# Two query groups per key chunk, and background matmuls in the column tiling of the values

## The chip, the cores and the metric

The kernel runs on one core of one Trainium2 chip. The metric is device time in microseconds (us). Five engines work side by side, each with its own instruction queue in program order: TensorE (PE, its weight loads shown apart as PEld), VectorE (DVE), ScalarE (ACT), GpSimd (POOL) and SyncE (SP), which here issues nearly all DMA transfers.

## The reference, cut to what matters

One transformer layer on x of 1 x 2048 x 640 in bf16: 32 heads of 20, then a gated bilinear feed-forward of width 1728.

```python
h  = x + softmax(q k^T * 20**-0.5) v @ wo      # q, k, v from layernorm(x) @ wqkv
n  = layernorm(h)
h2 = h + ((n @ w_gate) * (n @ w_up)) @ w_down
```

## The kernel before

**Names.** A head's 20 columns are padded to 32, so a group g of four heads fills 128 partitions; there are eight groups (G). A query chunk ci has 512, 512, 512, 256 and 256 queries (`CHUNKS`). A step is one group, one query chunk and 512 columns of scores per head: one key tile of 128 at 512 queries, two at 256. A bank is one head of a step, 128 x 512 scores in PSUM.

**A slot.** The main loop (from L802) runs slot by slot. `emit_exp` puts one ScalarE exponential on three banks, or on two, in turn; `emit_S` puts the score matmuls of a later unit on TensorE, four row tiles of 32; `values` and `emit_PV` multiply finished steps by V, four column tiles of 32 (out partitions 32 j to 32 j + 32, the extra column of ones in Vx giving the softmax sums). Some banks go another way: `start_D` and `pass_D` take the exponential on VectorE and GpSimd (fx, uc, v, ed). When a group's last key tile is through, `normalise` copies the sums (accS), sends them through DRAM to be inverted and spread (rs, rd, rb), and its `third` part writes `on`.

**The background.** Everything else is a generator in the deque `bg`, one matmul at a time, written into what the planner thinks is free TensorE time in a slot. `first_stage` normalizes the input chunk by chunk, transposes it (lnT), and makes K, Q and V: groups 0 and 1 padded (`proj_pad`), groups 2 to 7 densely (`proj_dense`), whose rows go from tmp to kT and qT by DMA on SP; `proj_v` makes V. `second_stage(ci)` is Wo, the second norm, gate and up (14 steps f), and down for a query chunk. Its matmuls are 128 x 128 wide. Generators run strictly one after the other.

**What sets the order.** The instruction order is fixed when the program is built, by running clocks (`pe_t`, `dve_t`, `act_t`), a credit for background work (`rate`) and `m_wait` for two PSUM banks (tag m). `need` breaks out of it: if a tag (a K, Q, V, or ("Wo", ci)) isn't done, it writes background work until it is, whatever the clocks say. A score needs K and Q, `third` of chunk ci needs ("Wo", ci - 1). `debt` writes matmuls of zeros that hold the clock up (L845). After chunk 0, `open_p2` opens the second stage's memory, clears wo on GpSimd and loads wo and Wd.

In chunk 0, group 0 goes through all 16 key tiles, then group 1, and so on:

```python
for g in range(G):
    for k0 in range(0, NT, nk):
        steps.append((ci, q0, qw, g, list(range(k0, k0 + nk))))
```

## Time and profile before

| | |
|---|---|
| median of 2 runs | 1076.33 us (1073.89 to 1078.76) |
| the profiled execution | 1075.21 us, of which the span is 1073.4 |
| mean granted TensorE clock | 0.938 |
| busy: PE, DVE, ACT, POOL | 906.2, 782.1, 865.6, 249.3 us |
| exponentials on ScalarE (L629) | 739, from 19.4 to 1016 us |
| instructions on TensorE in the order | 14,695 rows |

Rows of groups give line, engine, operation, tiles written and read, count, then busy us, mean ns of one, idle time before and what ended it. In a timeline row stand start, length, engine, line and count; in the chain of waits, start, length and what was waited for. A matmul's shape is followed by its tile in the array (rows*columns). Matmuls overlap, so a mean length is not a pace; the distance between starts is.

### The profile page before, as it was taken

What the parts mean: (1) busy time and instruction counts of PE and PEld (TensorE: products, weight loads), DVE (VectorE), ACT (ScalarE), POOL (GpSimd) and SP (SyncE); (2) the same over time, 40 slices, a digit from 0 to 9 for tenths busy, and PEclk for the clock granted to TensorE, in tenths of its full rate; (3) what the DMA queues carried; (4) which work ended last, traced back from release to release, by engine and by line L of the source; (5) the groups of instructions that cost most, each with busy time, mean ns of one, the idle gap of its engine ahead of it and who ended that gap; (6) DMA issues with size and microseconds to landing.
All of it is one profiled execution on the core that took longest, in us unless ns stands there. A gap on an engine that the chain in (4) does not pass through costs nothing.

```text
span 1073.4 us, 19367 instructions
## 1 busy us (share of the span) xinstructions
PE 906.2 (84%) x7249; PEld 349.3 (33%) x7348; DVE 782.1 (73%) x1327; ACT 865.6 (81%) x792; POOL 249.3 (23%) x273
## 2 busy tenths in 40 slices
PE   6778888888875888889888898898888889888968
PEld 2323233222221322233323222233333334434445
DVE  5426685778774899895888899966987886388532
ACT  4568795789884999999998999999968994289801
POOL 3002121222241322222322322222322230122100
PEclk8889799889986999999999999999988999989989
DMA  6200110110142222200012222000202222224145
GB/s 225 57 1 14 28 34 14 32 27 25 35 77 91 49 54 55 51 14 24 24 36 49 48 54 55 17 24 24 65 8 49 48 49 43 56 60 86 30 99 109
DMA packets 126860, 52.05 MB, mean 48 GB/s; under 512 B 108494, under 2 KB 121038, under 8 KB 126766
## 3 DMA queue, kind: packets, MB, share of 16 engines
q1 hardware_dynamic: 126078, 49.73, 19.8%
q8 instruction: 57, 0.93, 0.4%
q10 hardware_dynamic: 432, 0.98, 0.2%
q14 instruction: 37, 0.30, 0.1%
q0 software_dynamic: 256, 0.10, 0.0%
HBM read 43.60 MB, written 2.98 MB: 43 GB/s over the span
## 4 chain that ended last, share of the span: by engine, by line
ACT 39%; PE 24%; issue 18%; DVE 10%; DMA 4%; SPq 3%; POOL 1%; POOLq 0%; DVEq 0%; ACTq 0%
ACT E L629 38%; PE sp L609 6%; PE acc L706 3%; PE mt L547 3%; PE mt L301 2%; PE mt L520 2%; PE mt L360 2%; PE mt L529 2%; PE acc L845 2%; DVE v L662 2%; PE mt L488 2%; DVE ed L667 1%; DVE v L664 1%; SPq L350 1%; DVE st L222 1%
## 5 line engine op out<-in xcount | busy, mean ns | idle before, releaser
L629 ACT ACTIVATE E<-sp 128x1536 bf16<-128x1536 f32 x739 | 844.0, 1377 | 123.0 <-PE sp L609 103.3
L659 POOL TENSOR_SCALAR uc<-fx 128x512 f32<-128x512 uint16 x202 | 179.2, 887 | 584.9 <-DVE fx L656 576.1
L706 PE MATMUL acc<-E,Vx 128*32 128x512 bf16 (+1 forms) x2305 | 207.4, 357 | 5.6 <-DVE accS L720 3.6
L656 DVE TENSOR_SCALAR fx<-mt 128x512 int32<-128x512 f32 x202 | 137.6, 682 | 50.7 <-PE mt L609 49.5
L662 DVE SCALAR_TENSOR_TENSOR v<-fx 128x512 f32<-128x512 uint16 x202 | 168.7, 838 | 2.0
L664 DVE SCALAR_TENSOR_TENSOR v<-v,uc 128x512 f32<-128x512 f32 x202 | 142.9, 709 | 33.4 <-POOL uc L659 28.7
L667 DVE SCALAR_TENSOR_TENSOR ed<-fx,v 128x512 uint16<-128x512 int32 x202 | 143.4, 710 | 2.2
L706 PEld LDWEIGHTS <-Vx 128*32 128x32 bf16 x2560 | 57.3, 95 | 126.6 <-issue 122.2
L520 PE MATMUL mt<-ln2T,wg 128*128 128x512 bf16 (+3 forms) x328 | 83.7, 349 | 4.3 <-DVE ln2T L277 1.9
L529 PE MATMUL mt<-ln2T,wu 128*128 128x512 bf16 (+3 forms) x334 | 83.6, 345 | 2.8 <-issue 1.6
L706 PE MATMUL acc<-ed,Vx 128*32 128x512 bf16 (+1 forms) x255 | 78.9, 354 | 7.0 <-DVE ed L667 6.0
L547 PE MATMUL mt<-Wd,hh 128*128 128x320 bf16 x448 | 81.0, 302 | 1.7 <-DVE ot L552 1.7
L845 PE MATMUL acc<-zeros 128*128 128x512 bf16 x205 | 72.9, 425 | 2.4 <-issue 2.2
L741 POOL TENSOR_TENSOR on<-accS,rb 128x512 bf16<-128x512 f32 (+1 forms) x40 | 48.3, 1207 | 98.2 <-DMA rb<-rd 91.6
L488 PE MATMUL mt<-wo,on 128*128 128x320 bf16 x256 | 50.6, 328 | 19.8 <-POOL on L741 12.8
L535 DVE TENSOR_TENSOR hh<-gs,mt 128x512 bf16<-128x512 f32 (+1 forms) x70 | 40.4, 577 | 25.7 <-PE mt L529 24.6
L547 PEld LDWEIGHTS <-hh 128*128 128x128 bf16 x448 | 39.0, 97 | 40.6 <-issue 27.8
L520 PEld LDWEIGHTS <-wg 128*128 128x128 bf16 (+1 forms) x350 | 29.4, 101 | 40.6 <-issue 30.4
L277 DVE COPY gs<-mt 128x512 f32<-128x512 f32 (+3 forms) x56 | 34.7, 619 | 9.5 <-PE mt L520 8.6
L529 PEld LDWEIGHTS <-wu 128*128 128x128 bf16 (+1 forms) x350 | 29.0, 100 | 38.1 <-issue 27.1
L720 DVE COPY accS<-acc 128x512 f32<-128x512 f32 (+1 forms) x40 | 23.3, 583 | 24.2 <-PE acc L706 24.1
L552 DVE TENSOR_TENSOR ot<-mt,h 128x320 bf16<-128x320 f32 x32 | 15.6, 489 | 34.3 <-PE mt L547 34.2
(135 smaller groups left out, 934.8 us busy)
## 6 DMA issues: line engine op xcount, KB each, us to landing
wg<-in_B_w_gate_dram SPq DMA_DIRECT2D x65, 160.0 KB
wu<-in_B_w_up_dram SPq DMA_DIRECT2D x65, 160.0 KB
rb<-rd SPq DMA_DIRECT2D x24, 256.0 KB
out_dram<-ot SPq DMA_DIRECT2D x16, 160.0 KB
Wd<-in_B_w_down_dram SPq DMA_DIRECT2D x1, 2080.0 KB
rb<-rd SPq DMA_DIRECT2D x16, 128.0 KB
xr<-in_A_x_dram SPq DMA_DIRECT2D x3, 640.0 KB
rs<-accS SPq DMA_DIRECT2D x96, 2.0 KB
```

The source lines that it names most:

```text
L488: nc.tensor.matmul(ps[:, 0:HD], lhsT=On[ci, g][0][:, tt * P:(tt + 1) * P], rhs=wo[:, g, hsl], start=(g == 0), stop=(g == G - 1))
L520: nc.tensor.matmul(pg[0:M, 0:qw], lhsT=wg[:, c, 0:M], rhs=ln2T[:, c, 0:qw], start=(c == 0), stop=(c == KC - 1))
L529: nc.tensor.matmul(pu[0:M, 0:qw], lhsT=wu[:, c, 0:M], rhs=ln2T[:, c, 0:qw], start=(c == 0), stop=(c == KC - 1))
L547: nc.tensor.matmul(ps[:, 0:HD], lhsT=hh[f][0:K, tt * P:(tt + 1) * P], rhs=Wd[0:K, f, hsl], start=(f == 0), stop=(f == NF - 1))
L629: nc.scalar.activation(E[:, 0:len(u), :], sp[:, 0:len(u), :], ACT.Exp, scale=LN2_ / UNIT, bias=-BIAS * LN2_ / UNIT)
L656: nc.vector.tensor_scalar_mul(fx[:], d["sp"][:], 512.0)
L659: nc.gpsimd.tensor_scalar(d["uc"][:], u, EXP_C, 0.0, ALU.mult, ALU.add)
L662: nc.vector.scalar_tensor_tensor(d["v"][:], d["u"], EXP_A, d["u"], ALU.add, ALU.mult)
L664: nc.vector.scalar_tensor_tensor(d["v"][:], d["v"][:], EXP_B, d["uc"][:], ALU.add, ALU.mult)
L667: nc.vector.scalar_tensor_tensor(e[:], d["fx"][:], 1.0 / 512.0, d["v"][:], ALU.mult, ALU.add)
L706: nc.tensor.matmul(acc_t[32 * j:32 * j + 32, 0:qw], lhsT=Vx[:, kt, h * VS:h * VS + 32], rhs=E_of[s, j][0][:, i * qw:(i + 1) * qw], start=( ...
L845: nc.tensor.matmul(acc_t[:], lhsT=zeros[:, 0:P], rhs=zeros[:], start=False, stop=False, skip_group_check=True)
```

## The change

It has these parts.

- `cmm` writes a 128-wide matmul as four matmuls of 32 columns of weights, each into its own 32 partitions. All of the background but the transposes goes through it, the zeros of `debt` too.
- `steps`: in chunk 0, groups 0 and 1 take turns at each 512-key chunk, and accS collects their four partial sums (`ends`, `sums`). `first_stage` makes K of both groups and V of a chunk before the next chunk. While `ingest` holds, no exponential goes to VectorE; `on_act` sends no copy to ScalarE as long as exponentials are left.
- `values` writes two steps at a time (PVS); it also waits for V's copy.
- `third` doesn't call `need` early: it stays in `later` until its tags are done. The two chunks of 256 use two halves of `on` (`O0`, `free_of`), so that chunk 4 needs ("Wo", 0) to ("Wo", 2).
- The rate is RUSH0 = 10 in chunk 0 and while Wo runs (`hurry`); in the last two chunks it counts `more`, the work still to come. `bg` is written to pay `debt`, too, ahead of zeros.
- wo is loaded in `first_stage` over the first input tiles (tag xw), with its zeros by DMA; Wd is loaded in 14 pieces with the weights of chunk 0's second stage; xr and the output share two kept buffers.
- `more_banks` adds the five score banks to the ring of two before the first slot and after the last; 28 warm-up matmuls for 14.

```diff
+    def cmm(out, lhsT, rhs, start, stop, **kw):
+        m = lhsT.shape[-1]
+        for j in range(0, m, 32):
+            nc.tensor.matmul(out[j:j + 32], lhsT=lhsT[:, j:j + 32], rhs=rhs, start=start, stop=stop, **kw)
...
     def on_act(us):
-        return (n_slot < 40 or not left) and act_t + 0.4 < max(dve_t, pe_t)
+        return (not attn or not left or ingest and INGEST_ACT) and act_t + 0.4 < max(dve_t, pe_t)
...
         for ch in range(1, NCH):
-            for t in range(t0, t0 + TPC):
-                yield from proj_v(t, 0)
-                if lns is None:
-                    lns = finish(L, ch)
...
+            lns = finish(L, ch)
+            nxt = stats(ch + 1) if ch + 1 < NCH else None
             for i in range(TPC):
                 yield from transposed(lns[i], lnT_dst(ch * TPC + i))
+            for g in range(NG0):
+                yield from proj_pad(g, ch, 1)
                 if nxt is not None:
                     L = next(nxt)
+            for t in range(ch * TPC, (ch + 1) * TPC):
+                yield from proj_v(t, 0)
...
+        ingest = False
         fill_kq()
+        load_wo()
...
                 for f in range(NF):
-                    K = min(P, FF - f * P)
-                    nc.tensor.matmul(ps[:, 0:HD], lhsT=hh[f][0:K, tt * P:(tt + 1) * P],
-                                     rhs=Wd[0:K, f, hsl], start=(f == 0), stop=(f == NF - 1))
-                    pe(0.135)
+                    cmm(ps[:, 0:HD], hh[f][:, tt * P:(tt + 1) * P], Wd[:, f, hsl], f == 0, f == NF - 1)
+                    pe(0.135, "C")
...
-        for g in range(G):
-            for k0 in range(0, NT, nk):
-                steps.append((ci, q0, qw, g, list(range(k0, k0 + nk))))
+        order = [(g, k0) for k0 in range(0, NT, TPC) for g in range(NG0)] if ci == 0 else []
+        order += [(g, 0) for g in range(len(order) and NG0, G)]
+        for g, k0 in order:
+            k1 = k0 + TPC if ci == 0 and g < NG0 else NT
...
         def third():
-            if ci:
-                need(("Wo", ci - 1))
-            on = onp.tile([P, BK], BF16, name="on", tag=f"on{g}")
+            need(*[("Wo", c) for c in free_of[ci]])
+            on = ons[g]
...
+            if force is None and run == 0 and not ends[s][1]:
+                nxt = range(s, min(s + PVS, len(steps)))
...
-        while later and later[0][0] <= max(dve_t, act_t):
-            later.pop(0)[1]()
+        for z in list(later):
+            if z[0] <= max(dve_t, act_t) and all(t in done for t in z[2]):
+                later.remove(z)
+                z[1]()
...
+            more = sum(W1 * w / BK for w in CHUNKS[ci:-1]) if CHUNKS[ci] < BK else 0.0
             rest = sum(1 for b in left if steps[b[0]][0] == ci or CHUNKS[ci] < BK)
-            rate = RUSH * max(bgw, 5.0) / max(rest / 2.8, 4)
+            rate = RUSH0 if hurry or ci == 0 else RUSH * max(bgw + more, 5.0) / max(rest / 2.8, 4)
...
     values(len(steps))
+    more_banks()
```

Three places show how instructions move. On TensorE, in the down-projection of a chunk (Wd, hh), from the last score (sp) over the value group (acc) to the background (mt), before:

```order
L609 MATMUL sp<-qT_155,kT_151 128x512
L609 LDWEIGHTS kT_152
L609 MATMUL mt<-qT_155,kT_152 128x512
L706 LDWEIGHTS Vx
L706 MATMUL acc<-E,Vx 32x512
...
L547 LDWEIGHTS hh
L547 MATMUL mt<-Wd,hh 128x320
L609 LDWEIGHTS kT_151
L609 MATMUL sp<-qT_155,kT_151 128x512
```

and in the changed program:

```order
L684 LDWEIGHTS kT_150
L684 MATMUL sp<-qT_154,kT_150 128x512
L781 LDWEIGHTS Vx
L781 MATMUL acc<-E,Vx 32x512
...
L146 LDWEIGHTS hh_4780
L146 MATMUL mt<-Wd,hh_4780 32x320
```

Values and background now have one tiling; two value steps stand together, and a background matmul is four, with four loads. TensorE has 26,255 rows for 14,695.

On VectorE, while the last input chunk is normalized (x_101 before, x_100 after): lnT is its transposed copy; kT_146 before and kT_145 after are the keys of group 0, and kT_146 after those of group 1. Before:

```order
L241 RECIPROCAL rstd<-den 128x4
L246 TENSOR_SCALAR x_101<-x_101,mv,rstd 128x640 x4
L277 COPY lnT<-mt 128x5x128 x2
L315 TENSOR_SCALAR kT_146<-mt,kb 128x512
L656 TENSOR_SCALAR fx<-mt 128x512
L662 SCALAR_TENSOR_TENSOR v<-fx 128x512
```

and in the changed program:

```order
L261 RECIPROCAL rstd<-den 128x4
L266 TENSOR_SCALAR x_100<-x_100,mv,rstd 128x640 x4
L796 TENSOR_TENSOR accS<-accS,acc 128x512
L317 COPY lnT<-mt 128x5x128 x4
L354 TENSOR_SCALAR kT_145<-mt,kb 128x512
L796 TENSOR_TENSOR accS<-accS,acc 128x512
L354 TENSOR_SCALAR kT_146<-mt,kb 128x512
L317 CAST Vx<-mt 128x16x20 x4
```

All four transposed copies and the V casts of a chunk are VectorE's, the partial sums of both groups come in between, and the exponentials (fx, v) come later.

On VectorE at the end, from the last copy of sums (accS). Before:

```order
L720 COPY accS<-acc 128x256
L729 RECIPROCAL rr<-rs 128x8
L552 TENSOR_TENSOR ot<-mt,h 128x320 x3
L493 TENSOR_TENSOR h<-mt,xr 128x320 x4
L222 BN_STATS st<-h 128x6 x2
```

and in the changed program:

```order
L794 COPY accS<-acc 128x256
L813 RECIPROCAL rr<-rs 128x8
L317 COPY ln2T<-sp 128x5x128
L607 TENSOR_TENSOR hh_4771<-gs,sp 128x256
...
L607 TENSOR_TENSOR hh_4784<-gs,sp 64x256
L621 TENSOR_TENSOR xr<-sp,h 128x320 x3
L621 TENSOR_TENSOR xr<-mt,h 128x320
L566 TENSOR_TENSOR h<-mt,xr 128x320
```

Before, the end of chunk 3's down-projection (ot) stands behind the last sums, then Wo of chunk 4 (h). Now all 14 steps of chunk 3's gate and up (hh) and its down-projection (xr) stand there ahead of Wo. Behind the last value group TensorE has 1,676 matmuls for 273.

More of the change, by code (lines that the diff above doesn't have):

```diff
@@ L104 @@
     attn = False
+    hurry = False
+    ingest = True
     n_slot = 0
@@ L699, in emit_PV @@
         need(*[("V", kt, g // (G // 2)) for kt in kts])
-        first, last = kts[0] == 0, kts[-1] == NT - 1
+        first, last = ends[s]
         if first:
```

270 lines of the change are left out of this document (170 added, 100 removed).

## The prediction

> **What bounds the kernel now.** I read the page first, for the busy shares.
>
> ```profile
> span 1073.4 us, 19367 instructions
> PE 906.2 (84%) x7249; PEld 349.3 (33%) x7348; DVE 782.1 (73%) x1327; ACT 865.6 (81%) x792; POOL 249.3 (23%) x273
> L629 ACT ACTIVATE E<-sp 128x1536 bf16<-128x1536 f32 x739 | 844.0, 1377 | 123.0 <-PE sp L609 103.3
> ```
>
> TensorE and ScalarE are both near 80 to 85%, so an average names no bound. The third row says what can be lost: 739 exponentials, a slot each, and the idle time before them ends mostly with a score matmul (L609). Next I cut the span at the ends of stages and asked for the busy time and count of those exponentials in each (columns: length, ScalarE busy on that line and count, granted clock, DMA share, GB/s).
>
> ```profile
> 19.40:120.00 100.60, 59.40 (x51) 0.91 0.10 28
> 120.00:319.00 199.00, 168.29 (x147) 0.90 0.15 33
> 319.00:350.00 31.00, 14.76 (x14) 0.67 0.36 97
> 350.00:752.00 402.00, 392.82 (x348) 1.00 0.17 38
> 600.00:750.00 150.00, 150.00 (x134) 1.00 0.16 39
> 752.00:788.00 36.00, 28.76 (x26) 0.95 0.20 50
> 788.00:886.00 98.00, 89.03 (x79) 0.91 0.19 42
> 886.00:934.00 48.00, 14.11 (x14) 0.96 0.24 55
> 934.00:1016.00 82.00, 76.77 (x68) 0.94 0.28 58
> ```
>
> The stretch from 600 to 750 us is the yardstick: ScalarE never stops, 150.00/134 = 1.119 us a slot. Against it each stage loses its length minus 1.119 us times its count: 43.5 us while the input is read and normalized (19.4 to 120), 34.5 in the rest of chunk 0, 15.3 at the handover to chunk 1, 12.6 through chunks 1 and 2, 6.9 and 9.6 around chunk 3, 32.3 between 886 and 934, 5.9 to the end. That is 160.6; slots that cross a border are counted twice (747 for 739), which hides 9 more. So the span is 19.4 (start) + 739 x 1.119 = 827 + 169.6 lost + 57.4 of tail after the last exponential at 1016. ScalarE's pace bounds the middle; the rest is waiting.
>
> The largest wait, from the waits view, ScalarE's timeline and the chain:
>
> ```profile
> ACT E L629 <- PE sp L609: 103.3, 46, 33.9
> 932.45 4.62 ACT L629 ACTIVATE E<-sp 128x1536 bf16<-128x1536 f32 x4 [33.89 <-PE sp L609]
> 904.52 16.90 PE mt L547 x112
> 922.35 4.37 DMA xr<-in_A_x_dram
> 927.35 3.57 PE mt L488 x16
> 933.88 0.33 DVE accS L720
> ```
>
> In chunk 4, `third` needs the whole second stage of chunk 3 up to its Wo; that stands behind chunk 2's down-projection (112 matmuls at 16.90/112 = 0.151 us), so TensorE does it all at once while ScalarE idles 33.89 us.
>
> **The tiling change itself.** TensorE's timeline in a busy stretch (start, length, group):
>
> ```profile
> 501.30 0.39 PE L609 MATMUL sp<-qT_155,kT_152 32*128 32x512 bf16 x2
> 501.62 0.40 PE L706 MATMUL acc<-E,Vx 128*32 128x512 bf16 x4
> 501.95 0.55 PE L547 MATMUL mt<-Wd,hh 128*128 128x320 bf16 x2
> 502.64 0.39 PE L609 MATMUL sp<-qT_155,kT_152 32*128 32x512 bf16 x3
> ...
> 816.60 0.29 PE L706 MATMUL acc<-E,Vx 128*32 128x256 bf16 x2
> 816.60 0.28 PE L706 MATMUL acc<-ed,Vx 128*32 128x256 bf16 x1
> 816.61 0.39 PE L706 MATMUL acc<-E,Vx 128*32 128x256 bf16 x3
> 816.72 0.27 PE L706 MATMUL acc<-ed,Vx 128*32 128x256 bf16 x1
> 816.73 0.71 PE L706 MATMUL acc<-E,Vx 128*32 128x256 bf16 x17
> 817.37 0.39 PE L609 MATMUL sp<-qT_155,kT_149 32*128 32x256 bf16 x4
> ```
>
> Value groups are already four column tiles. Of the 24 from 816.60, the six groups take 0.77 us up to the next score. Four tiles start at one time, since six groups of 256 columns at the full pace of 0.109 us (which I estimate from 256 columns here: 0.77 less one changeover of 0.115, over 6) fit and 24 one behind another would not. A 512-column group is then about 0.216, and from a value group to the next background matmul it is 0.33 (501.62 to 501.95), so a changeover costs 0.33 - 0.216 = 0.115 us. The order has 1,856 changeovers before and 1,434 after: 422 x 0.115 = 48 us less of TensorE. A four-tile background group I price like the 128-wide matmul it replaces, because the value group has the same shape of load and output. But in chunks 1 and 2 ScalarE is busy 392.82 of 402 us, so there the 48 us only become slack. Slack of TensorE is not time.
>
> The Trainium skill speaks against the tiles: TensorEngine Tiling (Array Packing), section Tile-to-Partition Mapping, has column tiling switch off the fast weight load. The value rows carry such loads inside their 0.109 us, so here they stay hidden; if they did not, the result would be the slow rival below.
>
> **What moves, and its price.** The rest of the diff decides.
>
> Start and slots: 19.4 us as now; 740 exponentials for 739: 828.1.
>
> *Input stage (lost 43.5).* Now V casts and transposed copies also run on ScalarE between exponentials, and one group's 16 key tiles use up the chunks as fast as they come. After, VectorE takes all copies, and each 512-key chunk feeds two groups, 12.8 slots, 14.3 us. What stays is a forced lump at each new chunk.
>
> ```profile
> L720 DVE COPY accS<-acc 128x512 f32<-128x512 f32 x24 | 16.6, 690 | 17.3 <-PE acc L706 17.2
> L315 DVE TENSOR_SCALAR kT_147<-mt,kb 128x512 bf16<-128x512 f32 x4 | 3.0, 750 | 0.4 <-PE mt L301 0.3
> L277 DVE COPY lnT<-mt 128x640 bf16<-128x640 bf16 x6 | 3.0, 492 | 26.5 <-PE mt L292 26.5
> ```
>
> In VectorE's order (shown above) that is 0.69 + 4 x 0.492 + 0.75, with five K matmuls of 0.216 and about 0.8 of hops: 5.3 us. ScalarE has two units in hand (2.2), so 3.1 is lost three times, plus 3 to 4 for the clock, 0.91 in this stage: 13.
>
> *Rest of chunk 0 (34.5).* Groups 2 and 4 are scored as soon as their K and Q have passed through SP's queue:
>
> ```profile
> 298.89 4.48 SPq L350 DMA_DIRECT2D qT_155<-tmp  x6
> 1018.84 1.76 DMA rs<-accS
> ```
>
> That is 0.75 each to issue and 1.8 to land. Both early groups now end with the last key chunk, so group 2 waits for nine such issues: 0.9 + 9 x 0.75 + 1.8 = 9.5, less some 4.5 of matmuls planned in between and 2.2 in hand, about 3 to 4. Group 4 waits for 24 forced matmul groups (3.7) and eight issues: 3.7 + 0.9 + 6.0 + 1.8 - 2.2 = 10. The other four starts I take at 1.5 each. Sum 20.
>
> *Handovers.* `third` no longer forces Wo; it waits in `later` until Wo is done, and Wo runs with `hurry`. wo is loaded early and Wd in pieces. 15.3 becomes 5; 12.6, 6.9, 9.6 and 5.9, which hold smaller cases of it, become 9, 5, 8 and 6. Between 886 and 934 chunk 4's outputs lie in the other half of `on`, which only Wo of chunks 0 to 2 frees: 32.3 becomes 0. Lost after: 13 + 20 + 5 + 9 + 5 + 8 + 6 = 66.
>
> *The tail.* It grows. In the order all of chunk 3's feed-forward now stands behind the last value group, ahead of Wo of chunk 4.
>
> ```profile
> 1027.17 5.24 PE L488 MATMUL mt<-wo,on 128*128 128x320 bf16 x25 [2.51 <-POOL on L741]
> 1038.98 1.22 PE L520 MATMUL mt<-ln2T,wg 128*128 128x256 bf16 x5 [0.68 <-DVE ln2T L277]
> 1044.93 0.71 PE L520 MATMUL mt<-ln2T,wg 128*128 128x256 bf16 x5
> 1061.58 8.51 PE L547 MATMUL mt<-Wd,hh 128*128 128x320 bf16 x56
> ...
> 1052.59 4.78 DMA wg<-in_B_w_gate_dram
> ```
>
> Now: 11.2 until Wo, 11.8 to the first gate, 22.6 of gate and up, 8.5 of down, 3.3 to the end: 57.4. Eleven of the 14 steps run from 1044.93 to 1061.58, 1.5 us each. TensorE needs 10 x 0.109 = 1.09 for one, so weights (4.78 us for one transfer) set that pace, and seven PSUM banks instead of two do not mend it. After: 3 (transposes) + 21 + 8.5 for chunk 3, which covers the wait for `on`; then 10.9 (Wo at the full clock) + 21 + 8.5 + 3.3: 76. At TensorE's pace it is 64; with two weight loads in flight at 4.78 us, 2.4 a step, 101.
>
> Sum: 19.4 + 828.1 + 66 + 76 = 989.5, and 1.8 around the span (the profiled run took 1075.21 in all, 0.1% under the median of 1076.33): **992 us**, 8% faster.
>
> **Rivals.**
> (a) The first stages keep their losses: the lumps are serial through VectorE and SP's queue, and one late chunk delays both groups. For it: K and Q of each later group still pass SP one by one. Against: V casts leave ScalarE, and the lumps are short by their rows. Price 43.5 + 34.5 - 33 = 45: 1037.
> (b) The background tiles, with weights that change at every matmul, do not overlap. A group then costs four loads in turn:
>
> ```profile
> L706 PEld LDWEIGHTS <-Vx 128*32 128x32 bf16 x2560 | 57.3, 95 | 126.6 <-issue 122.2
> ```
>
> 4 x 0.095 = 0.38 in place of 0.109 to 0.216. By the order a 512-query stage holds 23 score groups (0.33 with their changeover), 16 value groups (0.216), 23 more changeovers and about 50 background groups (10 us): 23.7 us for ScalarE's 25.7. With 0.38 it is 32.7, +7 in 24 stages, 168. In chunks 3 and 4, 379 groups at +0.25 less their slack, about 62; 419 groups in the tail, 105: 1327, slower. TensorE passes ScalarE from about 0.25 a group on. Against it stands the row of 24 value matmuls.
> (c) TensorE's instruction supply. The program has 13,127 matmuls for 7,347. The densest 4 us stretch I found:
>
> ```profile
> 816.20:820.20 4.00, 3.76 (x64) 1.00 0.00 0
> ```
>
> That is 62.5 ns a matmul; bursts (24 in 0.77) may come out of a filled queue. If 62.5 ns were a limit, chunks 0 to 2 (7,901, 494 us of 621) would not feel it; chunks 3 and 4 (3,550) would need 222 us for 207, +15, and the tail (1,676) 105 for 63, +42: 1049. The Trainium skill, TensorE: Matmul & The Clock Gate, section "Wait — 56ns, not 53.3ns?", gives about 62 ns per matmul for one way of decoding and 25 ns otherwise; no run here shows which holds.
> (d) Losses fall to 40 (the handovers cost almost nothing) and the tail to 64: 954.
>
> **How the numbers follow.** Forecast 0.58, (a) 0.20, (b) 0.07, (c) 0.07, (d) 0.08. The forecast's own spread, 960 to 1025, comes from the tail's bounds and half the losses. The range 950 to 1050 takes in (a), (c) and (d) and leaves out (b) and edges of the others, under 2 in 10. About 2% is what a measurement of this kernel can tell: 1054.8 and 1097.9. Faster: the forecast, (d), nearly all of (a) and half of (c), 0.88. Slower: (b), 0.07. The same: 0.05.
>
> **What would show it.** Slots of 1.12 us in the middle with no wait over 6 us between 400 and 900; ScalarE lost about 13 us before the first dense projection and 10 at group 4; column-tiled groups of 512 starting 0.22 apart; the last exponential near 914; 76 us behind it, with weights as the releaser. I am wrong if background groups start over 0.25 apart, if the input stage still loses 40, or if the tail is far from 76.

## The result, and the profile after

The changed kernel takes 1041.54 us (1041.39 to 1041.69, two runs) for 1076.33: 0.9677 of the time before, 95% interval 0.9582 to 0.9771. Measured again beside other kernels it took 1044.9 us for 1077.62, 0.9687 (0.9657 to 0.9718). It is 3.2% faster where 8% was forecast; the time lies inside the range, 50 us above the forecast.

From the page of the changed kernel, span, busy times and the exponentials, now L704:

```profile
span 1039.9 us, 31066 instructions
PE 868.5 (84%) x13128; PEld 360.1 (35%) x13128; DVE 780.9 (75%) x1328; ACT 861.1 (83%) x784; POOL 234.1 (23%) x268
L704 ACT ACTIVATE E<-sp 128x1536 bf16<-128x1536 f32 x740 | 843.9, 1351 | 81.5 <-PE sp L684 47.7
```

TensorE's busy time fell by 37.7 us, the span by 33.5; both kernels keep TensorE busy 84% of the span. The idle time in front of the exponentials fell by 41.5. The same windows as before, cut at the new ends of stages (length, ScalarE busy on that line and count, granted clock, DMA share, GB/s):

```profile
21.90:109.00 87.10, 61.45 (x53) 0.89 0.18 43
109.00:293.00 184.00, 157.86 (x139) 0.93 0.13 32
293.00:321.00 28.00, 26.28 (x24) 0.94 0.11 35
321.00:726.00 405.00, 390.94 (x345) 0.98 0.19 44
726.00:766.00 40.00, 38.08 (x34) 0.96 0.21 49
766.00:878.00 112.00, 105.26 (x94) 0.92 0.21 46
878.00:942.00 64.00, 64.00 (x57) 1.00 0.15 39
```

The first stretch holds the start of group 2, which ScalarE's timeline shows beside the two waits of group 4:

```profile
106.14 1.02 ACT L704 ACTIVATE E<-sp 128x1024 bf16<-128x1024 f32 x1 [5.92 <-PE sp L684]
166.16 1.02 ACT L704 ACTIVATE E<-sp 128x1024 bf16<-128x1024 f32 x1 [4.96 <-PE sp L684]
172.08 1.45 ACT L704 ACTIVATE E<-sp 128x1536 bf16<-128x1536 f32 x1 [4.89 <-PE sp L684]
```

With 1.119 us a slot, as in the prediction, the sum compares so (lost = length less 1.119 us times count; the 5.9 us of group 2, which end inside the first window, are booked with the rest of chunk 0):

| term, us | forecast | measured | difference |
|---|---|---|---|
| start | 19.4 | 21.9 | +2.5 |
| 740 slots | 828.1 | 828.1 | 0 |
| input stage | 13 | 27.8 - 5.9 = 21.9 | +8.9 |
| rest of chunk 0 | 20 | 28.5 + 5.9 = 34.4 | +14.4 |
| handover 0 to 1 | 5 | 1.1 | -3.9 |
| chunks 1 and 2 | 9 | 18.9 | +9.9 |
| up to 766, up to 878 | 5 + 8 | 2.0 + 6.8 | -4.2 |
| up to the last exponential | 0 + 6 | 0.2 | -5.8 |
| six slots counted twice at borders | 0 | 6.7 | +6.7 |
| tail | 76 | 97.9 | +21.9 |
| span | 989.5 | 1039.9 | +50.4 |

The waits view of ScalarE (total, times, longest):

```profile
ACT E L704 <- PE sp L684: 47.7, 27, 5.9
ACT E L704 <- PE acc L781: 28.1, 20, 3.3
```

The wait of 33.9 us is gone; the longest is 5.9. The second row, exponentials that wait for value matmuls to free their buffers, was 10.3 before.

The tail by its parts: transposes, gate and up of chunk 3, down, Wo and layer norm of chunk 4, its gate and up, its down and the end (busy time of PE, PEld, DVE, ACT, POOL with counts, granted clock, DMA share, GB/s):

```profile
942.00:948.60 6.60, 1.29 (x16) 0.84 (x16) 2.42 (x6) 0.70 (x2) 1.03 (x2) 0.88 0.01 1
948.60:975.10 26.50, 20.07 (x540) 15.84 (x540) 5.52 (x14) 5.20 (x14) 0.73 (x1) 0.90 0.76 151
975.10:984.20 9.10, 8.09 (x236) 6.97 (x239) 1.91 (x5) 0.00 (x0) 0.00 (x0) 1.00 0.06 22
984.20:1001.50 17.30, 7.06 (x137) 4.85 (x127) 6.39 (x17) 0.69 (x1) 0.69 (x1) 0.71 0.41 86
1001.50:1028.00 26.50, 19.23 (x546) 15.99 (x547) 5.47 (x14) 5.20 (x14) 0.00 (x0) 0.93 0.63 133
1028.00:1039.90 11.90, 7.97 (x228) 6.38 (x219) 2.38 (x5) 0.00 (x0) 0.00 (x0) 0.97 0.08 29
```

And its timeline, at the first gate and in the middle of gate and up:

```profile
947.99 0.20 DVE L813 RECIPROCAL rr<-rs 128x8 f32<-128x8 f32 x1 [3.75 <-DMA rs<-accS]
948.11 0.47 DVE L317 COPY ln2T<-sp 128x640 bf16<-128x640 bf16 x1
948.63 1.26 PE L146 MATMUL sp<-ln2T,wg 128*32 128x256 bf16 x20 [3.47 <-DVE ln2T L317]
956.29 0.73 PE L146 MATMUL sp<-ln2T,wg 128*32 128x256 bf16 x20 [0.59 <-DVE hh_4773 L607]
957.49 0.73 PE L146 MATMUL sp<-ln2T,wu 128*32 128x256 bf16 x20 [0.47 <-ACT gs L313]
```

A reciprocal that waits 3.75 us for a transfer stands on VectorE ahead of the copy that the first gate needs. Further on, gate and up matmuls wait for the readers of other matmuls' results.

### The profile page after: what moved, and what is told of

The parts are those of the page before. It is cut to its first block, busy times and chain, and to the rows that moved or that the text cites. A ratio compares the mean times of both kernels' runs of the same rounds, so it can differ in the third digit from the quotient of the medians.

```text
span 1039.9 us, 31066 instructions
## 1 busy us (share of the span) xinstructions
PE 868.5 (84%) x13128; PEld 360.1 (35%) x13128; DVE 780.9 (75%) x1328; ACT 861.1 (83%) x784; POOL 234.1 (23%) x268
## 4 chain that ended last, share of the span: by engine, by line
ACT 37%; issue 25%; PE 18%; DVE 9%; DMA 5%; SPq 3%; POOL 2%; POOLq 0%; DVEq 0%; ACTq 0%
ACT E L704 37%; PE mt L146 7%; PE sp L684 5%; PE acc L781 3%; DMA rb<-rd 2%; SPq L389 2%; PE sp L146 2%; DVE v L737 2%; DVE v L739 1%; DVE fx L731 1%; DVE ed L742 1%; SPq L808 1%; DMA rs<-accS 1%; POOL uc L734 1%; PE acc L146 1%
## 5 line engine op out<-in xcount | busy, mean ns | idle before, releaser
L704 ACT ACTIVATE E<-sp 128x1536 bf16<-128x1536 f32 x740 | 843.9, 1351 | 81.5 <-PE sp L684 47.7
L734 POOL TENSOR_SCALAR uc<-fx 128x512 f32<-128x512 uint16 x198 | 170.2, 860 | 561.9 <-DVE fx L731 555.9
L781 PE MATMUL acc<-E,Vx 128*32 128x512 bf16 (+1 forms) x2312 | 166.5, 352 | 1.9 <-DVE accS L794 1.6
L739 DVE SCALAR_TENSOR_TENSOR v<-v,uc 128x512 f32<-128x512 f32 x198 | 141.7, 717 | 18.8 <-POOL uc L734 14.4
L146 PE MATMUL mt<-ln2T,wg 128*32 128x512 bf16 (+1 forms) x970 | 72.2, 376 | 2.8 <-DVE ln2T L317 1.0
L146 PE MATMUL mt<-ln2T,wu 128*32 128x512 bf16 (+1 forms) x970 | 70.8, 372 | 0.3 <-DVE gs L317 0.3
L146 PE MATMUL acc<-zeros 128*32 128x512 bf16 x696 | 63.1, 420 | 0.0
L146 PEld LDWEIGHTS <-wg 128*32 128x32 bf16 x1350 | 34.5, 99 | 42.7 <-issue 32.7
L146 PEld LDWEIGHTS <-wu 128*32 128x32 bf16 x1350 | 33.6, 98 | 33.3 <-issue 23.6
L684 PE MATMUL sp<-qT_154,kT_146 32*128 32x512 bf16 (+1 forms) x236 | 29.9, 335 | 13.9 <-ACT E L704 13.4
L684 PE MATMUL sp<-qT_154,kT_145 32*128 32x512 bf16 (+1 forms) x223 | 29.0, 343 | 11.4 <-ACT E L704 11.3
L684 PE MATMUL sp<-qT_154,kT_148 32*128 32x512 bf16 (+1 forms) x232 | 29.4, 341 | 10.7 <-ACT E L704 10.5
L794 DVE COPY accS<-acc 128x512 f32<-128x512 f32 (+1 forms) x40 | 23.2, 581 | 19.4 <-PE acc L781 16.9
L684 PE MATMUL sp<-qT_154,kT_152 32*128 32x256 bf16 (+1 forms) x232 | 27.8, 323 | 11.0 <-ACT E L704 10.6
L317 DVE COPY gs<-mt 128x512 f32<-128x512 f32 (+1 forms) x42 | 28.6, 682 | 8.2 <-PE mt L146 8.0
```

Of the source, the lines that this page charges most:

```text
L146: nc.tensor.matmul(out[j:j + 32], lhsT=lhsT[:, j:j + 32], rhs=rhs, start=start, stop=stop, **kw)
L317: nc.vector.tensor_copy(dst, src)
L684: nc.tensor.matmul(out[:, i * qw:(i + 1) * qw], lhsT=kT[g][32 * j:32 * j + 32, kts[i] * P:(kts[i] + 1) * P], rhs=q_of(g, q0, qw)[32 * j:32 ...
L704: nc.scalar.activation(E[:, 0:len(u), :], sp[:, 0:len(u), :], ACT.Exp, scale=LN2_ / UNIT, bias=-BIAS * LN2_ / UNIT)
L734: nc.gpsimd.tensor_scalar(d["uc"][:], u, EXP_C, 0.0, ALU.mult, ALU.add)
L739: nc.vector.scalar_tensor_tensor(d["v"][:], d["v"][:], EXP_B, d["uc"][:], ALU.add, ALU.mult)
```

## The experiments

One table for all runs; the edits follow. The ratio is to the kernel before, measured on the same chip. "Lost" is worked out from each trace: the time between the starts of the exponentials with the numbers given, less 1.119 us for each slot. Slot 60 lies a little behind the start of group 2, slot 195 at the end of chunk 0, slot 560 at the end of chunk 2. The tail runs from the end of the last exponential.

| kernel | median us | ratio (95%) | lost 0-60 | 60-195 | 195-560 | 560-end | tail |
|---|---|---|---|---|---|---|---|
| before | 1076.33 | 1 | 47.8 | 31.5 | 33.1 | 57.5 | 57.6 |
| after | 1041.54 | 0.9677 (0.9582-0.9771) | 28.9 | 30.1 | 20.7 | 12.1 | 97.9 |
| after_again | 1044.90 | 0.9687 (0.9657-0.9718) | 26.2 | 31.3 | 27.6 | 12.1 | 99.9 |
| wide_groups | 1051.13 | 0.9805 (0.9780-0.9831) | 30.8 | 29.3 | 28.5 | 11.9 | 97.1 |
| pvs1 | 1054.45 | 0.9774 (0.9744-0.9804) | 31.3 | 40.5 | 17.3 | 12.4 | 100.2 |
| wide_pvs1 | 1061.66 | 0.9895 (0.9832-0.9959) | 29.0 | 43.7 | 23.6 | 15.0 | 97.6 |
| before_tiles | 1057.17 | 0.9875 (0.9827-0.9922) | 39.2 | 29.0 | 27.0 | 53.2 | 59.0 |
| before_halves | 1073.50 | 1.0001 (0.9972-1.0030) | 47.2 | 34.5 | 31.9 | 17.5 | 94.5 |
| whole_on | 1047.72 | 0.9749 (0.9699-0.9799) | 30.6 | 27.8 | 24.8 | 47.4 | 65.3 |
| one_group | 1046.81 | 0.9701 (0.9652-0.9749) | 35.9 | 23.1 | 31.9 | 14.5 | 94.2 |
| ingest_act | 1088.87 | 1.0119 (1.0059-1.0178) | 66.6 | 28.2 | 26.0 | 17.3 | 96.8 |
| before_vcopies | 1062.77 | 0.9879 (0.9829-0.9929) | 51.1 | 23.5 | 32.4 | 51.6 | 56.6 |
| before_vcopies_tiles | 1073.37 | 0.9975 (0.9943-1.0007) | 48.2 | 30.4 | 35.0 | 50.9 | 57.4 |
| pool_q | 1041.12 | 0.9651 (0.9612-0.9690) | 26.1 | 27.2 | 28.0 | 9.7 | 96.7 |
| own_banks | 1032.67 | 0.9626 (0.9595-0.9657) | 28.9 | 31.0 | 27.8 | 12.4 | 85.1 |
| tail_all | 1030.63 | 0.9610 (0.9542-0.9677) | 25.3 | 30.9 | 22.7 | 11.7 | 85.7 |
| tail_res2 | 1020.64 | 0.9506 (0.9455-0.9556) | 29.4 | 29.6 | 30.3 | 12.5 | 71.2 |
| tail_res3 | 1016.95 | 0.9460 (0.9411-0.9508) | 30.4 | 29.5 | 27.6 | 10.3 | 65.5 |
| tail_warm | 1012.92 | 0.9415 (0.9369-0.9461) | 27.9 | 29.4 | 27.4 | 11.8 | 64.7 |
| tail_warm_pq | 1009.79 | 0.9389 (0.9337-0.9441) | 26.3 | 30.0 | 25.3 | 9.5 | 65.5 |

The yardstick, the changed kernel again:

> The changed kernel itself, as the yardstick for the others of this call. Every theory: its first figure, 1041.5, within the 4 us by which runs of the kernel before spread.

It came out at 1044.9, 3.4 us above its first figure. Between the two traces slots 195 to 560 differ by 7 us (20.7 and 27.6 lost) and slots 60 to 195 by 1.2, so a few us in the first of these columns show nothing.

### The tiling

wide_groups takes the column tiles back in the same order of instructions:

```diff
-        for j in range(0, m, 32):
-            nc.tensor.matmul(out[j:j + 32], lhsT=lhsT[:, j:j + 32], rhs=rhs, start=start, stop=stop, **kw)
+        nc.tensor.matmul(out[0:m], lhsT=lhsT, rhs=rhs, start=start, stop=stop, **kw)
```

> The changed kernel in the same order, with one 128-wide matmul wherever it issues four column tiles. Counted in the order, TensorE then changes its tiling 1,526 times for 1,433; 93 x 0.115 us is 11 us of TensorE. Theory (the tiles cost nothing and their saving is slack): 1041 to 1050, chunks 1 and 2 within 5 us of the changed kernel, the tail after the last exponential within 3 us of 97.9. Rival (four loads for one cost time): under 1030, with the tail at least 8 us shorter. Rival (the tiles are the gain): over 1065.

pvs1 writes values one step at a time:

```diff
-PVS = 2
+PVS = 1
```

> The changed kernel with values written one step at a time, not in pairs (PVS = 1); the order then holds 1,485 changes of tiling for 1,433, 6 us of TensorE. Theory (the pairs hold the exponentials' buffers too long): the waits of an exponential for a value matmul, 28.1 us in all, fall to 10 to 15, the slots of chunks 1 and 2 lose some 10 us for 18.9, and the time falls to 1030 to 1036. Rival (a value matmul is late because TensorE is behind, not because it waits for its pair): 1040 to 1050.

wide_pvs1 makes both edits:

> The changed kernel without anything on tiling: 128-wide background matmuls and values one step at a time. Its order holds 1,848 changes of tiling for 1,433: 415 x 0.115 = 48 us of TensorE. Theory of the prediction (only slack): 1040 to 1050. New theory (TensorE is the bound of chunk 0 and from chunk 3 on, and only chunks 1 and 2 have slack, so about half of the 48 us is time): 1060 to 1070. Rival (all of the change's gain is in the tiling): 1075 to 1080.

before_tiles puts only the tiles (with their mode "C" in the planner's clock) into the kernel before, here at the projections and so at every background matmul:

```diff
-            nc.tensor.matmul(ps[:], lhsT=lhs(c), rhs=lnT[:, c, sl],
-                             start=(c == 0), stop=(c == KC - 1))
-            pe(0.216)
+            cmm(ps[:], lhs(c), lnT[:, c, sl], c == 0, c == KC - 1)
+            pe(0.216, "C")
```

> The kernel before with nothing but the column tiles in its background (1,855 changes of tiling become 1,468: 387 x 0.115 = 45 us of TensorE). Theory (slack): 1062 to 1078, the 33.9 us wait of chunk 4 is still over 30. Rival (the tiles are the gain): 1041 or below. Rival (tiles cost time): over 1085.

Without anything on tiling the changed kernel is at 0.9895 for 0.9687: 2.1%, some 22 us of its gain of 34, go with the two edits together, and 1061.7 lies where the new theory put it (1060 to 1070). Its reason, changeovers in chunk 0, is not shown by that. The loss is there: slots 60 to 195 lose 43.7 us for 30.1 and 31.3 in the two executions of the changed kernel. But pvs1 alone loses 40.5 in them, and its trace counts 267 changes of tiling in that stretch for 264 (wide_pvs1: 322). What came in is two long waits of TensorE, for a transfer of K and for VectorE's exponentials (ed):

```profile
125.01 0.60 PE L684 MATMUL mt<-qT,kT 32*128 32x512 bf16 x1 [4.98 <-DMA kT<-tmp]
...
299.97 0.58 PE L781 MATMUL acc<-ed,Vx 128*32 128x512 bf16 x1 [6.62 <-DVE ed L742]
```

wide_pvs1 waits 4.73 and 5.29 us at the same two places; the changed kernel waits 0.80 us for the same transfer and 2.25 for the exponentials. So most of what this stretch loses comes with the order that the planner sets for single values, not with the number of changeovers. In slots 195 to 560 wide_pvs1 counts 899 changes for 710, which is 22 us of TensorE at 0.115, and loses 23.6 us for 20.7 and 27.6: in chunks 1 and 2 the saving is slack, as predicted. (The profiled execution of wide_pvs1 is 20 us above the first of the changed kernel and 12.5 us above that of after_again; where the rest lies is not shown.)

The tiles are tested cleanly by wide_groups alone, because only there the order stays. It is 1.2% slower than the changed kernel, about 12 us, a little beyond the 1041 to 1050 that slack allowed, so "only slack" does not hold for the whole kernel. Where the 12 us lie is not shown, as its profiled execution is no longer than that of after_again (spans of 1047.0 and 1047.4 us); and its order was laid out for the tiles, which may be part of it. The order holds 1,433 changes of tiling as it is, 1,526 with 128-wide groups, 1,485 with single values, 1,848 with both, so either one saves most of what the two save.

pvs1 is 0.9% slower. Both theories missed: the waits for value matmuls stayed (29.1 us for 28.1), so the pairs do not cause them, and the time went up, by the trace mainly through the two waits above.

before_tiles gained 1.25%, 13 us where pure slack gives none, 5 us below the 1062 to 1078 expected. Its trace lost less in every stretch of slots, most in the first (39.2 for 47.8); the wait of chunk 4 is 25.7 us for 33.9, where over 30 was expected. Its order was planned anew, so these 13 us are not the tiles' alone either (before_vcopies_tiles below has the same tiles and gains next to nothing).

### The wait of chunk 4

before_halves puts the halves of `on` into the kernel before, with O0 and free_of as the change computes them:

```diff
-            if ci:
-                need(("Wo", ci - 1))
-            on = onp.tile([P, BK], BF16, name="on", tag=f"on{g}")
-            nc.gpsimd.tensor_tensor(on[:, 0:qw], accS[:, 0:qw], rb[:, 0:qw], ALU.mult)
+            need(*[("Wo", c) for c in free_of[ci]])
+            on = ons[g]
+            nc.gpsimd.tensor_tensor(on[:, O0[ci]:O0[ci] + qw], accS[:, 0:qw], rb[:, 0:qw], ALU.mult)
```

> The kernel before with nothing but the halves of on (chunk 4 writes the half that Wo of chunks 0 to 2 frees). Theory: the wait of 33.9 us goes, and what TensorE did in it (down-projection of chunk 2, 16.9 us, and Wo of chunk 3) either fits the slack of the last 68 slots or comes back behind the last exponential, so the tail grows from 57.4 by 5 to 21: 1049 to 1066. Rival (the wait was worth all its length): 1042 to 1046 with the tail at 57. Rival (the work comes back whole as tail or as later stalls): over 1070.

whole_on takes them out of the changed kernel:

```diff
-        o0 = o0 if o0 + qw <= BK else 0
+        o0 = 0
```

> The changed kernel with the halves of on undone: every chunk writes columns from 0, so chunk 4 waits for Wo of chunk 3. Theory (TensorE works through that wait, so what it does there is missing from the tail): ScalarE loses 25 to 40 us in chunk 4, the tail falls from 98 to 55 to 72, and the time is within 8 us of the changed kernel, 1034 to 1052. Rival (the wait is time lost, as the prediction had it): 1060 or more.

The halves alone give nothing: 1.0001 (0.9972 to 1.0030). The slots win 37 us (the last exponential ends at 978.8 for 1015.8) and the tail gives 37 back (94.5 for 57.6). Of the two expectations, the rival that the work comes back whole was right. TensorE's side, first in the kernel before (columns as in the windows of the tail above):

```profile
886.00:934.00 48.00, 42.12 (x326) 21.34 (x333) 24.01 (x47) 14.11 (x14) 2.62 (x4) 0.96 0.24 55
...
sum 321.40, PE 271.19 PEld 126.54 DVE 216.76 ACT 214.56 POOL 61.88; mean PE 54.24 PEld 25.31 DVE 43.35 ACT 42.91 POOL 12.38
```

and in before_halves:

```profile
886.00:934.00 48.00, 41.73 (x535) 15.80 (x542) 40.85 (x68) 48.00 (x44) 12.98 (x14) 1.00 0.14 28
...
978.80:1073.30 94.50, 69.94 (x475) 44.12 (x472) 28.62 (x70) 11.85 (x31) 2.11 (x3) 0.89 0.58 109
sum 321.30, PE 268.79 PEld 122.67 DVE 208.31 ACT 222.50 POOL 65.14; mean PE 53.76 PEld 24.53 DVE 41.66 ACT 44.50 POOL 13.03
```

While ScalarE stood still between 886 and 934 us, TensorE was busy 42.12 of 48. From 752 us to the end it works 271 of 321 us in the one and 269 of 321 in the other. Only the place changes where ScalarE waits. The tail of before_halves holds 69.94 us of TensorE's work in 94.5, so it was not full there.

whole_on shows the same from the other side: the wait is back (25.2 us), the slots after 560 lose 47.4 for 12.1, the tail falls to 65.3, and the time is 0.6% above the changed kernel. So the halves are worth some 6 us there, not 32, and with intervals that overlap (0.9699 to 0.9799, 0.9657 to 0.9718) even these are not certain. What they are worth with the shorter tails below, no run shows.

### The first stage

one_group scores chunk 0 one group after the other, as before:

```diff
-        order = [(g, k0) for k0 in range(0, NT, TPC) for g in range(NG0)] if ci == 0 else []
+        order = []
...
-            k1 = k0 + TPC if ci == 0 and g < NG0 else NT
+            k1 = NT
```

> The changed kernel with the steps of chunk 0 ordered as before: all 16 key tiles of one group, then of the next, in place of two groups per key chunk; all else stays. Theory (the two groups per key chunk are what the first stage gained): the losses over the first 120 slots, 45 us in the changed kernel, go back towards the 67 of the kernel before, and the time to 1052 to 1065. Rival (the gain there is the tiles and the copies on VectorE): within 5 us of the changed kernel.

The theory fell: 0.9701 for 0.9687. Two groups per key chunk, by itself, gives nothing measurable. ScalarE then waits long, three times:

```profile
41.64 4.62 ACT L704 ACTIVATE E<-sp 128x1536 bf16<-128x1536 f32 x4 [13.39 <-PE acc L781]
...
58.37 8.23 ACT L704 ACTIVATE E<-sp 128x1536 bf16<-128x1536 f32 x7 [8.88 <-PE sp L684]
75.00 1.02 ACT L704 ACTIVATE E<-sp 128x1024 bf16<-128x1024 f32 x1 [8.41 <-PE sp L684]
```

and loses 35.9 us for 28.9 up to slot 60; but the next stretch gives it back (23.1 for 30.1), and by slot 195 both have lost 59.0 (over the 120 slots of the expectation, 45.6 for 45.3). The later groups start when the background has made their keys, and the order until then only sets where ScalarE waits: that is my reading of the equal sums.

ingest_act lets ScalarE copy out of PSUM in the input stage again:

```diff
-INGEST_ACT = 0
+INGEST_ACT = 1
```

> The changed kernel with ScalarE allowed to take copies out of PSUM in the input stage again, as in the kernel before. Theory of the prediction (such copies stand between the exponentials and cost slots there): the losses over the first 120 slots, 45 us, grow by 10 or more, 1052 to 1060. Rival (the stage ends when TensorE's background has made the keys of the third group, whoever copies): within 5 us of the changed kernel, 1039 to 1050.

before_vcopies forbids it in the kernel before, and before_vcopies_tiles adds the tiles to that:

```diff
-        return (n_slot < 40 or not left) and act_t + 0.4 < max(dve_t, pe_t)
+        return (not attn or not left) and act_t + 0.4 < max(dve_t, pe_t)
```

> The kernel before with nothing but this: once the exponentials run, VectorE takes every copy out of PSUM (ScalarE took them for the first 40 slots). Theory (ScalarE's copies stand between exponentials and starve TensorE, whose clock falls): the waits of Vx copies, 22.5 us, go, the first 120 slots lose 8 to 15 us less than 67, and the time is 1060 to 1068. Rival (the stage ends when the background has made the third group's keys, whoever copies; the changed kernel with such copies lost 45 us for a reason of its own order): within 5 us of the kernel before.

> The kernel before with both the column tiles in its background and the copies on VectorE. Theory (the two add): the 13 us of the tiles alone and what the copies alone give, 1047 to 1056, so that with the pairs of values and the halves little of the 34 us is left unexplained. Rival (both fill the same slack of the first stage): no more than 4 us below the better of the two alone.

In the changed kernel the copies' return costs 45 us, more than the whole gain: 38 of it lie in the first 60 slots (66.6 for 28.9; 83.0 for 45.3 over 120), far more than the expected 10. ingest_act, then the changed kernel, in one stretch (columns as in the windows of the tail):

```profile
60.00:105.00 45.00, 33.14 (x293) 11.07 (x293) 11.82 (x30) 24.95 (x27) 1.01 (x1) 0.58 0.00 1
```

```profile
60.00:105.00 45.00, 33.99 (x475) 14.39 (x474) 20.56 (x47) 32.84 (x29) 1.01 (x1) 0.95 0.03 6
```

TensorE is busy equally long, but at a granted clock of 0.58 it does 293 matmuls for 475. I read it so, without a run for it alone: a copy in ScalarE's queue waits for its matmuls and holds up the exponentials behind it, TensorE's scores wait for those (10.1 us in this stretch for 4.7), and the slow clock makes the next copy later. The edit also gives the planner another order.

From the kernel before, the copies alone give 1.2%, as expected (1062.8 for 1060 to 1068), but not in the input stage (51.1 us lost for 47.8; slots 60 to 195 lose 23.5 for 31.5; 63.8 for 66.8 over 120), and with the tiles together only 0.25%, with an interval that takes in no gain at all. Each alone gave 1.2%, so the two do not add, and the expected 1047 to 1056 was missed; since the planner orders everything anew with each edit, the parts of chunk 0 cannot be split further with these runs, and that stays open.

pool_q issues the moves of Q on GpSimd's queue:

```diff
-            nc.sync.dma_start(dst, tmp[lo - ft * P:hi - ft * P, 0:n])
+            eng = nc.gpsimd if b == 0 else nc.sync
+            eng.dma_start(dst, tmp[lo - ft * P:hi - ft * P, 0:n])
```

> The changed kernel with the moves of Q of the later groups issued by GpSimd's queue and only those of K by SP's. Theory (each group start waits for its row of issues at 0.75 us on one queue): the wait at 100 us (5.9) falls to 2 to 4, the second one at 167 us (4.9) to 1 to 3, and the time by 4 to 8 us, 1033 to 1038. Rival (landing or the matmuls in front set these waits): both stay within 1 us and the time at 1041, or above where GpSimd's own work is delayed.

Its waits at the same three places:

```profile
104.00 1.02 ACT L705 ACTIVATE E<-sp 128x1024 bf16<-128x1024 f32 x1 [4.53 <-PE sp L685]
166.88 1.02 ACT L705 ACTIVATE E<-sp 128x1024 bf16<-128x1024 f32 x1 [4.99 <-PE sp L685]
171.07 1.45 ACT L705 ACTIVATE E<-sp 128x1536 bf16<-128x1536 f32 x1 [3.17 <-PE sp L685]
```

5.92 became 4.53 and 4.89 became 3.17: the queue is part of these waits, less of it than expected. The time, 0.9651, is not clearly apart from 0.9687.

### The tail

own_banks replaces the slices behind the last exponential by five tiles of one bank each:

```diff
-    more_banks()
+    sA.release()
+    xb = tc.alloc_tile_pool(name="xb", bufs=1, space=PSUM)
+    for i in range(5):
+        ring.insert(i, dict(t=pe_t, ap=xb.tile([P, BK], F32, name=f"xb{i}", tag=f"xb{i}")[:]))
```

> The changed kernel with five separate one-bank tiles behind the last exponential in place of slices of a three-bank and a two-bank tile. Theory (a matmul into one slice waits for the reader of its neighbour): the 14 gate and up steps of chunk 3 and of chunk 4, 26.4 us each, fall to 17 to 21 us (1.1 to 1.5 a step, and the half-speed start), so 1025 to 1033. Rival (weights set the pace, as the prediction said): the steps stay above 24 us and the time within 4 us of 1041.5.

tail_all adds that chunk 3's transposes go ahead of `later`, and that xr of chunk 4 is loaded early:

```diff
+    need(("T", len(CHUNKS) - 2))
     while later:
...
+                if ci == len(CHUNKS) - 1:
+                    xrs[ci] = load_xr(ci, q0, qw)
                 bg.append(second_stage(ci, q0, qw))
```

> The changed kernel with one-bank tiles of its own behind the last exponential, chunk 3's transposes issued ahead of the last reciprocal on VectorE, and chunk 4's residual input loaded before chunk 3's feed-forward ends. Theory (each of the three waits is on the path of the tail): 98 us fall by 13 (banks, from the run of those alone), 3 to 4 (reciprocal) and 3 to 4 (input) to 77 to 80, the time to 1020 to 1027. Rival (the loads of weights take up what is won): 1030 to 1034, no better than the banks alone.

tail_res2 keeps the gate and up weights of the last two chunks in tiles that are done with: step g goes into kT[g] when group g of chunk 4 is done, steps 8 to 13 into qT1 behind the last value group. tail_res3, shown here, loads those six beside the others:

```diff
                 normalise(ci, q0, qw, g, sums.pop((ci, g)), t)
+                if ci == len(CHUNKS) - 1:
+                    load_res(g)
+                    if g < NF - G:
+                        load_res(G + g)
```

> As the kernel before it in this call, with the gate and up weights of the last two chunks loaded once into the keys' and queries' tiles that chunk 4 has done with, eight of the 14 steps while the attention still runs. Theory (weights set 1.45 us a step, TensorE needs 1.09): the two gate and up stretches fall from 24 and 22.5 to 16 to 19 us each, the time to 1010 to 1018. Rival (the loads delay the small transfers of the last outputs, or the half-speed start sets the stretch): 1020 or more.

> As the kernel with the weights loaded once, but all 14 steps' weights are loaded while the attention of chunk 4 still runs. Theory (the wait for a weight of 3.35 us at 966 us and the half-speed stretch behind it, 6 us for what takes 3, were the rest of the excess): chunk 3's gate and up fall from 22 to 16 us, the time from 1020.6 to 1012 to 1016. Rival (320 KB a group beside the attention delays its transfers): no gain, 1019 to 1025.

tail_warm puts matmuls on zeros into TensorE's wait for chunk 4's layer norm, and tail_warm_pq is that with pool_q's edit:

```diff
+        if ci == len(CHUNKS) - 1:
...
+            for _ in range(20):
+                nc.tensor.matmul(ps, lhsT=zeros[:, 0:P], rhs=zeros[:], start=True, stop=True)
...
```

> As the last kernel, and 20 matmuls on zeros (20 x 0.216 = 4.3 us) fill TensorE's wait for the layer norm of chunk 4. Theory (after that wait TensorE runs at half speed for some 4 us): the groups of chunk 4's first gate steps come 0.11 apart and not 0.21 to 0.25, 2 to 3 us less than the last kernel. Rival (the zeros end later than the layer norm, or the speed does not hang on what ran just before): the same or up to 2 us more.

> As the last kernel, with the moves of Q of the later groups on GpSimd's queue. Theory (that saved 3 to 4 us at the group starts, which reach the end): 3 to 4 us less than the last kernel, 1006 to 1012. Rival (its 0.4% was noise): the same within 2 us.

With own banks the waits for other matmuls' readers are gone. The waits for the layer norm (xr) and the transposes (ln2T) were there before; what is new in the tail is TensorE waiting for weights (wu):

```profile
PE xb L332 <- DVE xr L266: 7.0, 2, 6.0
PE xb L146 <- DVE ln2T L317: 4.3, 1, 4.3
PE xb L146 <- DMA wu<-in_B_w_up_dram: 3.3, 3, 1.3
```

The tail fell by 12.8 us (85.1 for 97.9), gate and up from 26.4 to 24.3 and 22.5 us each: less than the 17 to 21 expected, because now the weights set the pace, as the prediction had it: TensorE's weight loads wait 16.8 us for wg and wu, for 4.1 in the changed kernel. tail_all won nothing more (85.7). It moved a wait. Its first gate starts 3.1 us behind the last exponential, and the third step then waits for its weights:

```profile
954.38 1.26 PE L146 MATMUL mt<-ln2T,wg 128*32 128x256 bf16 x20 [5.62 <-DMA wg<-in_B_w_gate_dram]
```

With resident weights the tail is 71.2 us (tail_res2) and 65.5 (tail_res3). tail_res2, at 1020.6 us, missed its 1010 to 1018, and tail_res3 its 1012 to 1016 by 1 us. The step between the two is the wait that this row of tail_res2 shows, and the slow clock behind it:

```profile
966.64 1.26 PE L146 MATMUL xb<-ln2T,qT 128*32 128x256 bf16 x20 [3.35 <-DMA qT<-in_B_w_gate_dram]
```

tail_res3's TensorE, in chunk 3's gate and up and at the start of chunk 4's:

```profile
953.81 2.90 PE L146 MATMUL xb<-ln2T,kT 128*32 128x256 bf16 x100
956.54 1.26 PE L146 MATMUL mt<-ln2T,kT 128*32 128x256 bf16 x40
...
984.02 1.19 PE L332 MATMUL xb<-ident,xr 128*128 128x128 bf16 x10 [4.68 <-DVE xr L266]
985.80 2.33 PE L146 MATMUL mt<-ln2T,kT 128*32 128x256 bf16 x40 [0.58 <-DVE ln2T L317]
987.90 2.97 PE L146 MATMUL xb<-ln2T,kT 128*32 128x256 bf16 x100
```

100 matmuls take 2.73 us (953.81 to 956.54), 27 ns each, so a step is 1.09 us and chunk 3's gate and up 15.8 (951.07 to 966.9): TensorE's own pace, and 16 was expected. Behind a wait of 4.68 us, 40 matmuls take 2.10 us (985.80 to 987.90), 52 ns each, and the granted clock of that stretch is 0.50 (columns as in the windows of the tail):

```profile
985.80:987.90 2.10, 2.10 (x40) 1.56 (x44) 0.00 (x0) 0.37 (x1) 0.00 (x0) 0.50 0.00 0
```

In tail_warm:

```profile
978.48 4.49 PE L600 MATMUL xb<-zeros 128*128 128x512 bf16 x19
...
984.77 0.73 PE L146 MATMUL mt<-ln2T,kT 128*32 128x256 bf16 x20 [0.58 <-DVE ln2T L317]
985.33 2.90 PE L146 MATMUL xb<-ln2T,kT 128*32 128x256 bf16 x100
```

the first 20 take 0.56 us, 28 ns each: the full speed is kept. That is worth 1 us in the trace (40 x 25 ns; tails 65.5 and 64.7); the medians are 4 us apart with intervals that overlap, so more than 1 us is not shown. The same holds for tail_warm_pq, 3 us below tail_warm. At 1009.8 us it is 6.1% faster than the kernel before (0.9337 to 0.9441), well below the changed kernel, and the best kernel here.

## Why the prediction was wrong, and where it was right

The tail makes 21.9 of the 50 us by which the forecast was short, and the input stage, the rest of chunk 0 and chunks 1 and 2 make 33.2; the handovers came out 13.9 better. The rest is the start, 2.5, and a slip of the sum: before the change it added 9 us for slots counted twice at borders, after it none, and 6.7 were measured.

**"Between 886 and 934 ... 32.3 becomes 0."** The slots did win it, but the step booked a wait of ScalarE as time, without asking whether TensorE had any to spare. TensorE was busy 42 of those 48 us, and in the changed kernel it has no room ahead of the last exponential either:

```profile
878.00:942.00 64.00, 59.48 (x1238) 30.88 (x1233) 48.30 (x85) 64.00 (x57) 16.69 (x19) 1.00 0.15 39
```

So what it no longer does in the wait it does in the tail. The prediction had the tail grow by 19 us for it; it grew by 40. The halves are worth 0 alone and some uncertain 6 us with the rest, for a net 14 in the prediction.

**The tail, 76 forecast, 97.9 measured.** Its parts: 6.6 for 3 (the reciprocal ahead of the copy on VectorE), 26.9 and 26.5 for 21 each, 8.7 for 8.5, 17.3 for 10.9, 11.9 for 11.8. The mechanism named for gate and up, weights at 1.5 us a step, is the one that appears once the banks are separate (own_banks), and it goes when they are resident (tail_res3: 1.09, the TensorE pace the prediction had worked out). What was missed is that "seven PSUM banks" were slices of two tiles, so a matmul waits for the readers of its neighbour; that made the step 1.9 us, worse than the pace of two separate banks before.

**"But in chunks 1 and 2 ... the 48 us only become slack. Slack of TensorE is not time."** Right for those chunks: 189 more changes there cost wide_pvs1 no slots that can be seen. As a rule for the whole kernel it does not hold: the sum took nothing for the tiles anywhere, and wide_groups puts about 12 us on them. This miss has the other sign, since it makes the change better than forecast, so it is no part of the 50 us. The 422 changes are also not the tiles' alone: beside the pairs the tiles save 93.

**The input stage, 13 forecast, 21.9 measured.** The reasons were mixed up. That "each 512-key chunk feeds two groups" is worth nothing (one_group). That copies leave ScalarE matters in the changed order (ingest_act) and not in the old one, where this stage lost 51.1 us without them for 47.8 (before_vcopies). The price per lump was the wrong picture, and the 0.8 us of hops in it stands in no row: ingest_act's clock of 0.58 and one_group's equal losses point to a stage that ends when TensorE's background is through, however ScalarE spends the wait. No run tests that by itself.

**Rest of chunk 0, 20 forecast, 34.4 measured.** Group 4 came as worked out, 10 forecast and 4.96 + 4.89 measured. Group 2 took 5.9 for 3 to 4: its nine issues begin at 98.74 us, right behind four of the sums on the same queue (2.52 us), and TensorE's matmuls under them end at 100.46, 1.7 us for the 4.5 planned. "The other four starts I take at 1.5 each" leaves 6 for the remaining 18.6 us, and it looked in the wrong place. The two longest of the other waits, 2.60 us at 199.08 and 3.62 at 252.03, end with a score of a group that is already running, which stands behind a background matmul on TensorE; that one waits for VectorE to empty its bank (tmp), 1.79 and 3.46 us:

```profile
250.06 0.40 PE L146 MATMUL mt<-lnT,Wr_101 128*32 128x512 bf16 x4 [3.46 <-DVE tmp L373]
```

The prediction has no term for that. The rest is waits under 2 us, whose cause stays open.

**Chunks 1 and 2, 9 forecast, 18.9 measured.** The prediction took 3.6 us off ScalarE's old losses of 12.6; they grew. A part is in the waits for value matmuls, 6.2 us in the same chunks before and now:

```profile
ACT E L704 <- PE acc L781: 8.5, 8, 1.7
```

pvs1 rules out the pairs as the cause of such waits (10.1 us there with single values), and what it is stays open. In after_again, with the same waits for values (8.3), slots 195 to 560 lose 7 us more, so 18.9 is not a bad case.

**Handovers, 5 + 5 + 8 + 6 forecast, 1.1 + 2.0 + 6.8 + 0.2 measured:** right in kind, better than forecast.

**Rivals.** (b), tiles that do not overlap, and (c), 62.5 ns a matmul as a limit, are refuted by 100 matmuls in 2.73 us: four tiles with their own loads in 0.109 us, the price the prediction took. The Trainium skill, TensorEngine Tiling (Array Packing), section Tile-to-Partition Mapping, has column tiling switch off the fast weight load; wide_groups, the same order without column tiles, is not faster but 1.2% slower, so in sum that rule costs nothing here that can be seen. (a) named nearly the right time, 1037, for another reason: chunk 0 lost 56.3 us, half way between its 78 and the forecast's 33, and most of the rest of the gap is the tail, which (a) left at 76. (d) is refuted: losses and tail are both larger.

## What to carry to other kernels

Before a wait is booked as time won, look at what the engine it waits for does meanwhile: if that is busy through the wait and nearly full from there to the last slot, the work only moves, and the end shows it. Where two edits remove the same changeovers, test each without the other before crediting either, and count the changeovers in the stretch that got slower. Where a planner sets the order, an edit also makes another order, and that alone can cost or win 1% (pvs1; before_tiles and before_vcopies with both together); only an edit that keeps the order tests a mechanism cleanly. In this tail a new wait stood behind each one removed (banks, then weights, then the clock), so such fixes are worth measuring together.

## What the runs showed of the hardware that was not expected

- TensorE kept up 27 ns a matmul over 100 column-tiled matmuls, each with its own load (tail_res3). The Trainium skill, TensorE: Matmul & The Clock Gate, section "Wait — 56ns, not 53.3ns?", gives a floor of about 25 ns and 62 ns for one way of decoding; 27 lies just above the first, and 62 did not bind.
- A granted clock of 0.58 over 45 us of a stage with TensorE busy 74% of the time (33.14 of 45 us), for 0.95 at nearly the same busy time: that an engine is busy does not show that it is fast.
- 52 ns for 27 over the first 40 matmuls behind a wait of 4.68 us, at a granted clock of 0.50, and 28 ns when matmuls on zeros filled the wait. The same page's Part 1 on the clock gate has an idle TensorE throttled to half and activity release it; these rows agree.
